# Windowed attention and a gated feed-forward on one core: two heads in one full-array matmul over 64-key blocks

## The chip, the cores and the metric

The kernel runs on one core of one Trainium2 chip. The metric is the device time of one execution in microseconds (us): the median of three runs. A profile of one execution is taken beside it, on the same chip, and all views quoted below are read from that trace.

## The reference, cut to what matters

Attention over 8 batches, 8 heads, 576 tokens and 64 dimensions a head, with two kinds of causal window, and then a gated feed-forward over all 4608 tokens:

```python
scores = scale * np.matmul(q, k.transpose(0, 1, 3, 2))
rel = pos[:, None] - pos[None, :]
mask_plain = (rel >= 0) & (rel < 32)                       # heads 0 to 3
mask_dil = (rel >= 0) & (rel < 128) & (rel % 4 == 0)       # heads 4 to 7
scores = np.where(mask, scores, -1e9)
attn = exp(scores - max); attn = attn / sum(attn)
attn_out = np.matmul(attn, v)                              # 8 x 8 x 576 x 64
x = attn_out.transpose(0, 2, 1, 3).reshape(4608, 512)
g = x @ w_gate                                             # 512 -> 1536
val = x @ w_val
return (gelu(g) * val) @ w_out                             # 1536 -> 512
```

A query of a plain head sees itself and the 31 tokens before it. A query of a dilated head sees every fourth token, 32 of them: sorted into four classes by position modulo 4, it sees itself and the 31 before it in its own class of 144 tokens. So most of the 576 x 576 scores of a head need not be computed.

## The kernel before

The tokens go through the feed-forward in nine blocks (`c`) of 512. A block has a gate stage, 96 matmuls of 512 columns (12 groups `nb` of 8), and an output stage, 48 matmuls (four rows of tokens `tb`, twelve terms `fc`). The attention of later batches is woven into these stages: `n` counts pairs of heads, four to a batch (two plain, two dilated), 32 in all. For each pair there is a score stage (`emit_s`), an exponential on ScalarE, a mask multiply on VectorE, and a value stage (`emit_pv`) with the denominators (a matmul with ones) and the numerators. Then VectorE transposes the denominators in 32x32 squares, takes reciprocals of one column of each, transposes them back and scales the numerators into `xT`, the feed-forward's input.

The two heads of a pair stand in the two halves of the array. In the score stage they use the upper and the lower 64 rows, as a head has 64 dimensions; in the value stage the left and the right 64 columns:

```python
def emit_s(n, b0, pe_mask=False):
    ...
    if is_plain(n):
        ...                                   # pe_mask: the mask as a bias, by matmuls with the identity
        for j in (0, 1, 2, 3, 4):             # 128-key blocks, 160 queries each
            for hl in range(2):
                kt = qtp_[64 * hl : 64 * hl + 64, 1, hp, :]
                qt = qtp_[64 * hl : 64 * hl + 64, 0, hp, :]
                ...
                mm(ps[:, bank, c0 : c0 + w], kt[:, k0 : k0 + P], qt[:, q0 : q0 + w], ...)
        nc.scalar.activation(pt[:, :, 0:PB], ..., AF.Exp, ...)          # 960 columns
        nc.scalar.activation(pt[:, :, PB:PH], ..., AF.Exp, ...)         # 384 columns
    else:
        ...                                   # 12 matmuls in halves: 8 of 128 columns, 4 of 32
        nc.scalar.activation(pt, ps[:, b0 : b0 + 4, 0:DW], AF.Exp, ...) # 1152 columns
    def emit_mask():
        nc.vector.tensor_tensor(pt, pt, mb, ALU.mult)

def emit_pv(n, b0, parts=("den", "num"), wide=False, flip=False):
    ...                                       # about 20 matmuls with 64 weight columns each
    for o, lhs, rhs, st in mms:
        nc.tensor.matmul(o, lhs, rhs, start=st, stop=True, skip_group_check=True)

def emit_both(n, b0):                         # plain pairs in a gate stage: values and ones side by side
    for hl in range(2):
        for j in range(5):
            ...                               # 128 weight columns: 64 of values, 64 of ones
            nc.tensor.matmul(ps[...], trio[:, hl : hl + 2, :]..., pt[:, hl, p0 : p0 + w], ...)
```

A batch is loaded two blocks ahead: plain q, k and v as float32 by the sync engine's queue and cast by GpSimd; the dilated parts by GpSimd's own queue, which casts on the way; then q and k are turned by DMA transposes:

```python
def load_batch_rest(b):
    st, sv = tiles["plain", b]
    qd, rd = load_qk_dil(b)
    qp = cast_qk_plain(b, st)
    load_v_dil(b)
    v_cast(b, sv)
    ...
    nc.sync.dma_start_transpose(out=dst[:, :, 0:P], in_=qd...)
    nc.sync.dma_start_transpose(out=dst[:, :, P:NCL], in_=rd...)
    for kb in range(5):
        nc.sync.dma_start_transpose(out=..., in_=qp[0:n, kb]...)
    last_keys(b, 0, HK, nc.gpsimd)
```

Which pair stands where is given by small tables. The plain pairs of batches 4 to 7 and the last dilated ones have their value stages in gate stages (`values_a`), the others in output stages (`values_b`):

```python
scores = {1: range(8, 12), 2: range(12, 17), 3: range(17, 22), 4: range(22, 27), 5: range(27, 32)}
values_b = {1: range(8, 12), 2: range(12, 16), 3: range(17, 20), 4: range(22, 24), 5: range(27, 28)}
values_a = {3: {4: 16}, 4: {2: 20, 6: 21}, 5: {1: 24, 4: 25, 7: 26}, 6: {1: 28, 4: 29, 7: 30, 10: 31}}
biased = (9,)
```

Of the kernel before, what the change touches and what calls it, by code (L numbers as in the profile page):

```python
# [21 lines left out]
def kernel(  # L22
# [14 lines left out]
    P = 128  # L37
# [13 lines left out]
    PB = 3 * PW  # L51
    PH = PB + P + PT
# [6 lines left out]
    qtp = ctx.enter_context(tc.tile_pool(name="qtp", bufs=2))  # L59
    prb = ctx.enter_context(tc.tile_pool(name="prb", bufs=8))  # L60
    nrm = ctx.enter_context(tc.tile_pool(name="nrm", bufs=2))
    ffn = ctx.enter_context(tc.tile_pool(name="ffn", bufs=3))
    osbp = ctx.enter_context(tc.tile_pool(name="osbp", bufs=4))
# [4 lines left out]
    mask_p = const.tile([P, PH], F16, tag="mask_p")  # L68
    mask_d = const.tile([P, DW], F16, tag="mask_d")
    bias_p = const.tile([P, PH], F16, tag="bias_p")  # L70
    bias_d = const.tile([P, DW], F16, tag="bias_d")
# [7 lines left out]
    vset = [  # L79
        (  # L80
            const.tile([P, 4, HP, 3, D], F16, tag=f"vp{i}", name=f"vp{i}"),
            const.tile([P, HK, 4, D], F16, tag=f"vd{i}", name=f"vd{i}"),
            const.tile([P, HP, 3, D], F16, tag=f"vt{i}", name=f"vt{i}"),
            const.tile([P, HK, 2, D], F16, tag=f"vr{i}", name=f"vr{i}"),
        )
        for i in range(3)
    ]
# [100 lines left out]
    def new_qt(b):  # L188
        tiles["qT", b] = (
            qtp.tile([P, 2, 2, S], F16, tag="qTp", name=f"qTp{b}"),  # L190
            qtp.tile([P, 2, HK, 2, NCL], F16, tag="qTd", name=f"qTd{b}"),
            qtp.tile([P, HK, 2, 64], F16, tag="kTr", name=f"kTr{b}"),
        )

    def new_v(b):

        sv = ldp.tile([P, 5, HK, D], F32, tag="sv", name=f"sv{b}")
        tiles["v", b] = vset[b % 3]
        return sv
# [18 lines left out]
    def load_qk_plain(b):  # L218
        st = ldp.tile([P, 5, 2, HK, D], F32, tag="st", name=f"st{b}")
        for t, src in ((0, q), (1, k)):  # L220
            for kb in range(5):
                n, sr = rows(src, b, kb)
                gated(nc.sync.dma_start(out=st[0:n, kb, t], in_=sr))
        return st

    def cast_qk_plain(b, st):
        qp = ldp.tile([P, 5, 2, HK, D], F16, tag="qp", name=f"qp{b}")
        nc.gpsimd.tensor_copy(qp[:, 0:4], st[:, 0:4])  # L228
        nc.gpsimd.tensor_copy(qp[0:64, 4], st[0:64, 4])
        return qp  # L230

    def load_qk_dil(b):
        qd = ldp.tile([P, 2, HK, 4, D], F16, tag="qd", name=f"qd{b}")
        rd = ldp.tile([16, 2, HK, 4, D], F16, tag="rd", name=f"rd{b}")
        for t, src in ((0, q), (1, k)):
            nc.gpsimd.dma_start(out=fl(qd[:, t]), in_=quads(src, b, HK, 0, 4 * P))
        for t, src in ((0, q), (1, k)):
            nc.gpsimd.dma_start(out=fl(rd[:, t]), in_=quads(src, b, HK, 4 * P, S))
        return qd, rd

    def load_eights(b):
        q8 = ldp.tile([R8, 2, HK, 8, D], F16, tag="qd", name=f"qd{b}")
        for t, src in ((0, q), (1, k)):
            tiles["last"] = nc.gpsimd.dma_start(
                out=q8[:, t].rearrange("p h r d -> p h (r d)"), in_=eights(src, b, HK, H)
            )
        return q8
# [12 lines left out]
    def load_batch_plain(b):  # L260
        st = load_qk_plain(b)
        sv = new_v(b)
        v_plain(b, sv, nc.sync)
        return st, sv

# [4 lines left out]
    def load_batch_rest(b):  # L270
        st, sv = tiles["plain", b]
        qd, rd = load_qk_dil(b)
        qp = cast_qk_plain(b, st)
        load_v_dil(b)
        v_cast(b, sv)
        new_qt(b)
        qtp_, qtd_, _ = tiles["qT", b]
        dst = qtd_.rearrange("p t h m i -> p (t h m) i")
        nc.sync.dma_start_transpose(out=dst[:, :, 0:P], in_=qd.rearrange("p t h r d -> p (t h r d)"))
        nc.sync.dma_start_transpose(out=dst[:, :, P:NCL], in_=rd.rearrange("p t h r d -> p (t h r d)"))  # L280
        dst = qtp_.rearrange("p t h c -> p (t h) c")
        for kb in range(5):
            n = min(P, S - kb * P)
            nc.sync.dma_start_transpose(
                out=dst[:, :, kb * P : kb * P + n], in_=qp[0:n, kb].rearrange("p t h d -> p (t h d)")
            )
        last_keys(b, 0, HK, nc.gpsimd)

# [51 lines left out]

    def emit_s(n, b0, pe_mask=False):
# [5 lines left out]
        if is_plain(n):  # L349
# [18 lines left out]
            pt = prb.tile([P, 2, PH], F16, tag="P", name=f"P{n}")  # L368
# [4 lines left out]
        else:  # L373
# [17 lines left out]
            pt = prb.tile([P, 4, DW], F16, tag="P", name=f"P{n}")  # L391
# [82 lines left out]
    def emit_both(n, b0):  # L474


        b, hp = n // NHP, n % 2
        pt = tiles["P", n]
        vp, _, vt, _ = tiles["v", b]
        for hl in range(2):  # L480
            for j in range(5):
                w = (PW, PW, PW, P, PT)[j]
                p0 = j * PW - (32 if j == 4 else 0)
                trio = vp[:, j, hp] if j < 4 else vt[:, hp]
                nc.tensor.matmul(
                    ps[:, b0 + 2 * hl + j // 4, j % 4 * P : j % 4 * P + w],
                    trio[:, hl : hl + 2, :].rearrange("p x d -> p (x d)"),
                    pt[:, hl, p0 : p0 + w],
                    start=j in (0, 4),
                    stop=True,  # L490
                    skip_group_check=True,
                )

    def both_rows(half, b0, hl):
        return psf[64 * half : 64 * half + 64, (b0 + 2 * hl) * 512 : (b0 + 2 * hl) * 512 + S]

    def norm_both_r(n, b0):
        dt = nrm.tile([P, 18, 32], F32, tag="dt", bufs=1)
        for hl in range(2):
            nc.vector.transpose(  # L500
                dt[64 * hl : 64 * hl + 64].rearrange("p b c -> p (b c)"), both_rows(1 - hl, b0, hl)
            )
        recip(n, dt)

    def norm_both_x(n, b0):
        b = n // NHP
        rb = tiles.pop(("rb", n))
        for hl in range(2):
            half = slice(64 * hl, 64 * hl + 64)
            nc.vector.tensor_tensor(  # L510
                xT[pair(n)][half, b * S : (b + 1) * S], both_rows(hl, b0, hl), rb[half], ALU.mult
            )

# [52 lines left out]
    def norm_parts(n, b0, at):  # L566

        for q0, q1 in ((0, at), (at, S)):
            dt = nrm.tile([P, 18, 32], F32, tag="dt", bufs=1)
            dt = dt[:, 0 : (q1 - q0) // 32]  # L570
            c0 = b0 * 512 + 960
            nc.vector.transpose(dt.rearrange("p b c -> p (b c)"), psf[:, c0 + q0 : c0 + q1])
            recip(n, dt)
            dst = xT[pair(n)][:, n // NHP * S + q0 : n // NHP * S + q1]
            num = psf[:, b0 * 512 + q0 : b0 * 512 + q1]
            nc.vector.tensor_tensor(dst, num, tiles.pop(("rb", n))[:, 0 : q1 - q0], ALU.mult)
# [82 lines left out]

    for vp_, _, vt_, _ in vset:  # L660
        nc.vector.memset(vp_.rearrange("p j g x d -> p (j g) x d")[:, :, 1, :], 1.0)
        nc.vector.memset(vt_[:, :, 1, :], 1.0)
# [11 lines left out]
    first_vd = ldp.tile([P, HK * 4 * D], F32, tag="st", name="st0")  # L674
    nc.sync.dma_start(out=fh(first_vd), in_=quads(v, 0, HK, 0, 4 * P))
    q6 = ldp.tile([R6, 2, 6, HK, D], F16, tag="qp", name="qp0")
# [57 lines left out]
    st1 = ldp.tile([R6, 2, HK, 6 * D], F32, tag="st", name="st1")  # L734
# [7 lines left out]
    q61 = ldp.tile([R6, 2, 6, HK, D], F16, tag="qp", name="qp1")  # L742
    for hp in range(2):
        for t in range(2):
            cast_six("pool", q61, st1, t, hp)
    gate["dma"] = wo1
    v_plain(1, sv1, nc.sync)
    v_cast(1, sv1)
    tiles["plain", 2] = load_batch_plain(2)

    mm0 = 0

    scores = {1: range(8, 12), 2: range(12, 17), 3: range(17, 22), 4: range(22, 27), 5: range(27, 32)}
    values_b = {1: range(8, 12), 2: range(12, 16), 3: range(17, 20), 4: range(22, 24), 5: range(27, 28)}
    values_a = {3: {4: 16}, 4: {2: 20, 6: 21}, 5: {1: 24, 4: 25, 7: 26}, 6: {1: 28, 4: 29, 7: 30, 10: 31}}
    biased = (9,)

    places = {
        1: "0.0m 1.3v 1.3s 1.3x 1.3m 2.5v 2.5s 2.5x 2.5m 3.0s 3.0m 3.6v 3.6x 3.12w",
        2: "0.0m 1.3v 1.3s 1.3x 1.3m 2.5v 2.5s 2.5x 2.5m 3.0s 3.0m 3.6v 3.6s 3.6x 3.12w 3.12m",
        3: "0.0m 1.3v 1.3s 1.3x 1.3m 2.5v 2.5s 2.5x 2.5m 2.11s 2.11m 3.6v 3.6s 3.6x 3.6m",
        4: "0.0m 1.3v 1.3s 1.3x 1.3m 2.4v 2.4s 2.4x 2.4m 2.11s 2.11m 3.7s 3.7m",
        5: "0.0m 1.3v 1.3s 1.3x 1.3m 2.1s 2.1m 2.10s 2.10m 3.6s 3.6m",
    }
    places = {c: [(int(w[0]), int(w[2:-1]), w[-1]) for w in p.split()] for c, p in places.items()}
    late = False
    for c in range(NCH):  # L770
# [87 lines left out]
        else:  # L858
# [39 lines left out]
            if lone:  # L898
                gelu_table()
# [36 lines left out]
```

The softmax here doesn't subtract the row's maximum and nothing guards it: scores larger than these inputs give would overflow.

## Time and profile before

| What | Value |
|---|---|
| Device time, median of 3 runs (lowest to highest) | 348.68 us (348.41 to 349.46) |
| Gate matmuls, 128x512, one of the two matrices | x432, 114.0 us busy |
| Output matmuls, 128x512 | x420, 96.9 us busy |
| Exponential, dilated pair, 1152 columns | 1130 ns |
| Exponential, plain pair, 960 and 384 columns | 970 and 488 ns |
| Mask multiply, dilated and plain pair | 751 and 856 ns |
| Transposes of denominators and of reciprocals, 576 columns | 778 ns each |
| Scaling into xT, dilated and plain pair | 1129 and 749 ns |
| DMA transposes of q and k on the sync queue (dilated, its rest, plain) | x6, x6, x30 |

Line numbers (L584) are those of the kernel printed above: L584 is a gate matmul, L618 an output matmul, L360 and L390 are scores, L472 and L485 values. "PE" is TensorE's matmuls, "PEld" its weight loads, "DVE" VectorE, "ACT" ScalarE, "POOL" GpSimd, "SPq" the sync engine's DMA queue. In a timeline a line has the start in us, the length in us, engine, line, operation, shapes and count. The length of a matmul contains its way through the array, so matmuls overlap one another; the distance between starts is what one costs.

### The profile page before, as it was taken

To read this page: it belongs to the slowest core of one execution; us is meant where nothing else is said; L and a number is where in the kernel's file an instruction comes from. 1 tells how busy PE (TensorE), PEld (TensorE's weight loads), DVE (VectorE), ACT (ScalarE), POOL (GpSimd) and SP (SyncE) were. 2 spreads that over 40 slices of the span, in tenths; PEclk is the share of its full clock that TensorE was granted. 3 is DMA by queue.
4 is the path that set the end of the run, shared out by engine and by line. 5 is a ranking of instruction groups with operands and counts; after the bars stand their busy time and mean duration, and the time that the engine had idled before them with its cause. 6 is when DMAs were issued, how large, how long until landed. Compare 5 with 4: busy or idle time off the path is not lost.

```text
span 347.0 us, 6006 instructions
## 1 busy us (share of the span) xinstructions
PE 336.0 (97%) x2342; PEld 163.7 (47%) x2342; DVE 201.8 (58%) x309; ACT 148.2 (43%) x220; POOL 84.0 (24%) x123
## 2 busy tenths in 40 slices
PE   8879999999999999999999999999999999999996
PEld 3644454444544445444544454444444444444443
DVE  3784488443794359674878576975498423303320
ACT  1753473535543447336553547336633223223321
POOL 8893304630630540351006300510000000000000
PEclk9999999999999999999999999999999999999999
DMA  8999999999999999898169925991100020020002
GB/s 179 225 201 223 205 200 192 184 147 258 178 107 256 191 152 171 201 162 121 62 159 168 157 73 137 195 126 55 70 0 0 32 91 1 2 91 30 2 30 91
DMA packets 107516, 44.44 MB, mean 128 GB/s; under 512 B 83328, under 2 KB 102912, under 8 KB 107488
## 3 DMA queue, kind: packets, MB, share of 16 engines
q1 hardware_dynamic: 84192, 31.01, 39.2%
q0 software_dynamic: 22752, 12.33, 28.9%
q10 hardware_dynamic: 544, 0.72, 0.8%
q8 instruction: 18, 0.29, 0.4%
q14 instruction: 10, 0.08, 0.1%
HBM read 39.85 MB, written 9.44 MB: 142 GB/s over the span
## 4 chain that ended last, share of the span: by engine, by line
PE 70%; DVE 13%; DMA 10%; issue 3%; ACT 2%; SPq 1%; POOL 1%; DVEq 0%; POOLq 0%; ACTq 0%
PE ps L584 42%; PE ps L618 21%; PE ps L472 4%; DMA st<-in_k_dram 4%; DMA sv<-in_v_dram 3%; DMA wv<-in_moe_w_val_dram 3%; DVE dt L500 2%; DVE dt L533 2%; DVE u_all L607 2%; DVE xT L559 2%; DVE rb L544 2%; DVE P L400 2%; DVE xT L510 1%; PE ps L390 1%; DVE rc L542 1%
## 5 line engine op out<-in xcount | busy, mean ns | idle before, releaser
L607 DVE SCALAR_TENSOR_TENSOR u_all<-g,ps 128x512 f16<-128x512 f16 x108 | 72.8, 684 | 76.7 <-PE ps L584 67.9
L606 ACT ACTIVATE g<-ps 128x512 f16<-128x512 f32 x108 | 63.9, 596 | 123.3 <-PE ps L584 122.8
L584 PE MATMUL ps<-xT,wg 128*128 128x512 f16 x432 | 114.0, 379 | 1.2 <-POOL xT L707 0.7
L584 PE MATMUL ps<-xT,wv 128*128 128x512 f16 x432 | 113.8, 379 | 0.2 <-DVE u_all L607 0.2
L618 PE MATMUL ps<-wo,u_all 128*128 128x512 f16 x420 | 96.9, 380 | 0.2 <-DVE qTd L303 0.2
L584 PEld LDWEIGHTS <-wv 128*128 128x128 f16 x432 | 42.2, 98 | 52.8 <-issue 2.9
L584 PEld LDWEIGHTS <-wg 128*128 128x128 f16 x432 | 41.3, 98 | 48.9 <-issue 1.1
L618 PEld LDWEIGHTS <-u_all 128*128 128x128 f16 x420 | 38.4, 98 | 44.7 <-issue 0.8
L629 ACT ACTIVATE osb<-ps 128x512 f32<-128x512 f32 x33 | 19.7, 597 | 38.8 <-PE ps L618 37.8
L228 POOL CAST qp<-st 128x2048 f16<-128x2048 f32 x6 | 11.4, 1893 | 97.8 <-DMA st<-in_k_dram 64.8
L544 DVE STREAM_TRANSPOSE rb<-rc 128x576 f32<-128x576 f32 (+4 forms) x34 | 25.3, 743 | 1.3
L533 DVE STREAM_TRANSPOSE dt<-ps 128x576 f32<-128x576 f32 x21 | 16.3, 778 | 12.4 <-PE ps L472 12.3
L392 ACT ACTIVATE P<-ps 128x1152 f16<-128x1152 f32 x16 | 18.1, 1130 | 11.8 <-PE ps L390 11.8
L370 ACT ACTIVATE P<-ps 128x960 f16<-128x960 f32 x16 | 15.5, 970 | 11.0 <-PE ps L360 11.0
L559 DVE TENSOR_TENSOR xT<-ps,rb 128x576 f16<-128x576 f32 x16 | 17.9, 1129 | 2.2 <-PE ps L472 1.9
L400 DVE TENSOR_TENSOR P<-P,mask_d 128x1152 f16<-128x1152 f16 x13 | 9.8, 751 | 9.7 <-ACT P L392 9.7
L400 DVE TENSOR_TENSOR P<-P,mask_p 128x1344 f16<-128x1344 f16 x14 | 11.8, 856 | 2.9 <-ACT P L371 2.9
L472 PE MATMUL ps<-P,ones 128*64 128x96 f16 (+5 forms) x174 | 11.3, 244 | 2.1 <-DVE P L400 1.5
L472 PEld LDWEIGHTS <-ones 128*64 128x64 f16 x174 | 7.2, 109 | 11.5 <-issue 8.6
L631 DVE TENSOR_SCALAR osb<-ps 128x512 f32<-128x512 f32 x2 | 1.4, 691 | 18.2 <-PE ps L618 18.2
L255 POOL DMA_DIRECT2D vr<-in_v_dram x16 | 9.9, 632 | 5.3 <-DMA wv<-in_moe_w_val_dram 3.6
L500 DVE STREAM_TRANSPOSE dt<-ps 64x576 f32<-64x576 f32 x14 | 10.9, 781 | 0.4
(88 smaller groups left out, 247.8 us busy)
## 6 DMA issues: line engine op xcount, KB each, us to landing
out_dram<-osb SPq DMA_DIRECT2D x35, 256.0 KB, 2.0
sv<-in_v_dram SPq DMA_DIRECT2D x40, 128.0 KB, 3.3
st<-in_q_dram SPq DMA_DIRECT2D x24, 128.0 KB, 3.1
st<-in_k_dram SPq DMA_DIRECT2D x24, 128.0 KB, 3.1
vd<-in_v_dram POOLq DMA_DIRECT2D x7, 256.0 KB, 6.5
wo<-in_moe_w_out_dram POOLq DMA_DIRECT2D x3, 512.0 KB, 19.7
qd<-in_q_dram POOLq DMA_DIRECT2D x6, 256.0 KB, 5.4
qd<-in_k_dram POOLq DMA_DIRECT2D x6, 256.0 KB, 6.9
```

The costliest lines, as they stand in the source:

```text
L392: nc.scalar.activation(pt, ps[:, b0 : b0 + 4, 0:DW], AF.Exp, bias=0.0, scale=scale)
L400: nc.vector.tensor_tensor(pt, pt, mb, ALU.mult)
L472: nc.tensor.matmul(o, lhs, rhs, start=st, stop=True, skip_group_check=True)
L500: nc.vector.transpose(dt[64 * hl : 64 * hl + 64].rearrange("p b c -> p (b c)"), both_rows(1 - hl, b0, hl))
L533: nc.vector.transpose(dst, den)
L544: nc.vector.transpose(rb[:, 0 : 32 * nb].rearrange("p (b c) -> p b c", c=32), bass.AP(tensor=rc.tensor, offset=rc.offset, ap=[rc.ap[0], [1 ...
L559: nc.vector.tensor_tensor(dst.rearrange("p (i m s) -> p i m s", m=2, s=2), num, rb.rearrange("p (s m i) -> p i m s", s=2, m=2), ALU.mult,)
L584: nc.tensor.matmul(ps[:, bank, :], w[:, kc, ns], xT[kc][:, tok], start=first, stop=end)
L606: nc.scalar.activation(g, ps[:, banks[0], :], AF.Gelu)
L607: nc.vector.scalar_tensor_tensor(u_all[:, nb, :], g, USCALE, ps[:, banks[1], :], ALU.mult, ALU.mult)
L618: nc.tensor.matmul(ps[:, bank, :], u_all[:, fc, tb * P : (tb + 1) * P], wo_t[fc // 4][:, fc % 4, :], start=(fc == 0), stop=(fc == NNB - 1),)
L629: nc.scalar.activation(osb, ps[:, bank, :], AF.Copy, bias=0.0, scale=1.0 / USCALE)
```

## The change

For batches 2 to 7 a pair's two heads go through the array together. The keys come in blocks of 64. A weight tile has one head's 64 keys in its first 64 columns and the other's in the last, each over its own 64 rows, and zeros in the other two quarters; so one matmul on the full array gives both heads' scores. Values are laid out the same way, and a matrix of ones in two diagonal squares gives the denominators. This takes less masked area (96 queries to 64 keys where it was 160 to 128), one exponential and one mask multiply of 832 or 768 columns to a pair, and no half-array form. Batches 0 and 1 keep the old form.

```diff
+    BK, BQ = 64, 96
+    LP, LD = 8 * BQ + BK, 4 * (BQ + 80) + BK
...
+    def two_s(n, bank):
...
+        for e, c0, t0, w in two_blocks(n):
+            if is_plain(n):
+                mm(c0, w, kp[:, 2 * e + hp, :], qp[:, hp, t0 : t0 + w])
+            else:
+                r = e % 4
+                mm(c0, w, kd[:, e, :], qd[:, hp, r, t0 - NCL * r : t0 - NCL * r + w])
+        if not is_plain(n):
+            mm(LD - BK, BK, kd[:, 16 + hp, :], qd[:, hp, :, P:NCL])
+        pt = prb.tile([P, LP], F16, tag="P", name=f"P{n}")
+        nc.scalar.activation(pt[:, 0:ln], psf[:, base : base + ln], AF.Exp, bias=0.0, scale=scale)
...
+    def two_m(n):
+        nc.vector.tensor_tensor(pt, pt, mask, ALU.mult)
...
+    def two_den(n, i):
+        two_mms(n, win(n, i), None)              # ones; several blocks in one matmul
+    def two_num(n, i):
+        ...                                      # one matmul a block, two where a bank ends
```

All loads of these batches now go through the sync engine's queue as float32, into a stage of three parts that is used twice a batch, and GpSimd casts them into the block-diagonal tiles; keys are transposed with their zeros:

```diff
+    def load_first(b):
+        load_q_plain(b, 0)                       # 6 loads
+        load_two(k, b, 1, True)                  # 4
+        load_q_dil(b, 2)                         # 1
+        cast_q_plain(b, 0)
+        cast_two(k16[:, 0], 1)
+        load_two(k, b, 0, False)                 # 6
+        cast_q_dil(b, 2)
+        cast_two(k16[:, 1], 0)
+    def load_rest(b):
+        if b < 5:
+            zero(blocks(vraw[b % 3], 1)), zero(blocks(vraw[b % 3], 0))
+        turn(qp..., q16[:, 0:1280])              # 10 blocks of 128 columns
+        turn(kp, k16[:, 0]...)                   # 18
+        load_two(v, b, 1, True)                  # 4
+        cast_two(vp, 1)
+        turn(qd..., q16[:, 1280:2304])           # 8
+        load_two(v, b, 2, False)                 # 6
+        cast_two(vd, 2)
+        turn(kd, k16[:, 1]...)                   # 18
+        nc.gpsimd.tensor_copy(qd[:, :, :, P:NCL], ...)
```

(The counts behind # are added here.) The tables are replaced by a list for each stage. A number is so many feed-forward matmuls; S, M, D, N are scores, mask, denominators and numerators of a pair; T is the first transpose with the reciprocal, B the second transpose, X the scaling; g and u are the two halves of the gating, e a store. What follows @ is the window in PSUM that the stage uses:

```diff
-    values_a = {3: {4: 16}, 4: {2: 20, 6: 21}, 5: {1: 24, 4: 25, 7: 26}, 6: {1: 28, 4: 29, 7: 30, 10: 31}}
+    gates = {
...
+        3: (
+            "G 2 T15 2 N15@1 e3@2 1 B15 3 X15 4 D16@0 N16@1 T16 2 g0 2 g1 1 u0 2 u1 2 g2 1 B16 3 u2 3 X16 1 g3 4 "
+            "u3 4 g4 4 u4 ..."
+        ),
...
+    outs = {
+        1: (
+            "9 S8@0 11 e0@1 M8 2 S9@0 1 D8@0 N8@1 T8 2 e1@1 1 S10@0 M9 1 B8 3 D9@0 X8 2 S11@0 M10 2 T9 N9@1 3 M11 "
+            "e2@1 1 D10@0 B9 2 T10 4 X9 2 N10@0 1 B10 1"
+        ),
+        2: (
+            "1 u11 6 S12@2 11 e0@2 M12 2 S13@2 1 D12@1 N12@0 T12 3 S14@2 M13 e1@2 1 B12 3 D13@1 X12 2 S15@2 M14 2 "
+            "T13 N13@0 3 M15 1 D14@1 B13 e2@2 S16@2 T14 5 X13 1 N14@1 1 B14 2 D15@0 M16 2 X14 1"
+        ),
...
```

So values that stood in the middle of gate stages now stand in output stages and in the first part of the gate stage after, and a store's fourth part (e3) of a block is issued in the next block, behind the loads of a batch. Masks, stages and tiles of probabilities share memory with others (the first batches' probabilities lie in the unused end of `xT`), and there are three output buffers in place of four.

## The prediction

> **What bounds the kernel now.** I read the busy shares first, then the table by stage, then the chain of waits piece by piece, then single stretches of TensorE's timeline, and last the DMA queue that the sync engine issues. The page says who is full:
>
> ```profile
> span 347.0 us, 6006 instructions
> PE 336.0 (97%) x2342; PEld 163.7 (47%) x2342; DVE 201.8 (58%) x309; ACT 148.2 (43%) x220; POOL 84.0 (24%) x123
> PEclk9999999999999999999999999999999999999999
> ```
>
> TensorE is busy 97% of the span at its full granted clock, so a time can only fall if TensorE gets less to do or idles less. How much of either there is, the last two blocks show. They hold no attention work, and the chain of waits has them as bare matmul stretches:
>
> ```profile
> 281.44 20.80 PE ps L584 x96
> 302.24 10.36 PE ps L618 x48
> ```
>
> One block of 512 tokens costs 20.80 + 10.36 = 31.16 us of feed-forward matmuls, 144 of them at 0.216 us. Nine blocks are 280.4 us and the change touches none of them. What it can touch lies in blocks 1 to 6. From TensorE's timeline I took where each block's first gate matmul starts (62.1, 98.9, 136.7, 173.9, 210.9, 247.5, 281.4) and asked for the table by stretch:
>
> ```profile
> 62.10:98.90 36.80, 36.56 (x276) 17.65 (x272) 20.27 (x29) 17.05 (x25) 14.62 (x19) 1.00 1.15 181
> 98.90:136.70 37.80, 36.90 (x284) 17.81 (x278) 23.27 (x37) 18.52 (x29) 12.00 (x17) 1.00 0.99 182
> ...
> 173.90:210.90 37.00, 36.26 (x261) 17.80 (x260) 26.99 (x39) 18.18 (x27) 8.85 (x12) 1.00 0.72 135
> ...
> sum 219.30, PE 216.62 PEld 105.27 DVE 143.83 ACT 100.65 POOL 50.67; mean PE 36.10 PEld 17.55 DVE 23.97 ACT 16.77 POOL 8.45
> ```
>
> The columns are length, then busy time of TensorE, its weight loads, VectorE, ScalarE and GpSimd. The six blocks take 219.3 us. Six times 31.16 is 187.0, so batches 2 to 7 cost 32.3 us beside the feed-forward: 219.3 - 216.6 = 2.7 us idle and 29.6 us of attention on TensorE. That is the whole pot, 9% of the time.
>
> Next, how attention is paid for now. Four lines of TensorE's timeline around one score and one value stage in half arrays:
>
> ```profile
> 157.84 1.03 PE L584 MATMUL ps<-xT,wv 128*128 128x512 f16 x4
> 158.79 0.47 PE L360 MATMUL ps<-qTp 64*128 64x160 f16 x10
> 159.19 3.41 PE L618 MATMUL ps<-wo,u_all 128*128 128x512 f16 x15
> 162.53 0.56 PE L472 MATMUL ps<-P,ones 128*64 128x64 f16 x10
> ```
>
> And three lines of it around a value stage on the full array:
>
> ```profile
> 145.16 1.03 PE L584 MATMUL ps<-xT,wv 128*128 128x512 f16 x4
> 146.03 0.43 PE L485 MATMUL ps<-P,vp 128*128 128x160 f16 x4
> ...
> 146.61 1.03 PE L584 MATMUL ps<-xT,wg 128*128 128x512 f16 x4
> ```
>
> Durations overlap, so starts are to be subtracted. From 157.84 to 158.79 are 0.95 us for four matmuls worth 0.86: entering the half-array form costs 0.09 us. From 159.19 to 162.53 are 3.34 us for fifteen worth 3.24: again 0.10. On the full array, from 145.16 to 146.03 are 0.87: nothing. The ten plain score matmuls (1344 columns) take 159.19 - 158.79 = 0.40 us, less than the 0.57 us that 1344 columns cost at 0.423 ns (0.2167 us over 512), so the two halves do run side by side. The full-array value stage runs 1344 columns in 0.58 us, exactly at that rate.
>
> **What the Trainium skill says.** "TensorEngine Tiling (Array Packing)", Tiling Modes, says that independent tiles work in parallel but that changing the tiling mode drains the engine; the trace agrees with both, 0.40 us against 0.57 for the parallel part and 0.09 to 0.10 us for the drain. "TensorE: Matmul & The Clock Gate", Back-to-back issue gap, gives about 81 ns per 128-column matmul with its own weight load in a stream; this trace differs, since ten matmuls of 134 columns on average took 58 ns each, and it decides. "VectorE: DVE Perf Modes", section on mode 2x_1P, allows two 16-bit results a cycle for a two-tensor operation on packed data; the mask multiplies agree (1152 columns in 751 ns, 1344 in 856: 0.55 ns a column and 0.12 fixed), so a shorter mask is worth what its columns are.
>
> **The change part by part.** A 64-key block with its two heads block-diagonal has 832 columns for a plain pair (eight of 96, one of 64), 768 for a dilated pair (four of 96, four of 80, 64 for the rest), each for scores, denominators and values.
>
> Price of a small full-array matmul. The page has no 96-column one with 128 weight columns, so I estimate from the transposes: twelve of 96 columns between 43.56 and 44.17 us, less a drain of 0.1, are 42 ns; twenty-four of 72 columns between 13.40 and 14.28 are 37 ns. I take 42 ns for 96, 40 for 80, 37 for anything shorter, and 0.423 ns a column where several blocks share one matmul (the denominators).
>
> - Plain pair: scores 8 x 42 + 37 = 0.37; denominators 832 x 0.423 = 0.35; values, where a bank border cuts one block, 7 x 42 + 3 x 37 = 0.41. Sum 1.13 us.
> - Dilated pair: scores 4 x 42 + 4 x 40 + 37 = 0.37; denominators 768 x 0.423 = 0.33; values 0.33 + 2 x 37 = 0.40. Sum 1.10 us.
> - Twelve of each: 26.8 us, in place of 29.6. TensorE saves 2.8 us.
>
> Where the 2.8 come from: the score stages drop from 0.49 (0.40 + 0.09) and 0.46 to 0.37 each, 24 x 0.105 = 2.5; the plain value stages in halves drop from 0.90 (0.80 + 0.10) to 0.76, five of them, 0.7; the four bias matmuls of one pair go, 0.6; the seven plain value stages that were already on the full array get dearer, 0.58 to 0.76, minus 1.3; dilated values stay (0.74 before with the drain, 0.73 now). The sum is 2.5, near the 2.8 by subtraction. This is the point of the estimate: zeros are multiplied now, and the parallel halves were worth nearly as much as the drains they cost.
>
> VectorE. A plain pair now costs mask 832 columns 0.58, transpose 0.78, reciprocal 0.27, transpose 0.78, scaling 0.76: 3.2 us; a dilated one 0.54 and 1.13 in place of 0.58 and 0.76: 3.5. The seven pairs of the gate stages cost 0.86 + 1.59 + 0.27 + 0.78 + 1.53 = 5.0 before. Over all, about 7 x 1.8 + 17 x 0.2 = 16 us less of VectorE, off the path except at the tight places. ScalarE's exponential goes from 1.13 or 1.35 us to about 0.85. Neither engine becomes the bound over a block (27 busy us of 37 at most before).
>
> Tight places stay. Between one pair's denominators and the next pair's values in the same two banks, VectorE needs 0.78 + 0.27 + 0.58 + 0.78 + 1.13 = 3.5 us and five hand-overs; the new lists put eleven 0.216-us matmuls and four small stages of 0.35 to 0.41 between, 3.9 us. At a block's end a queued transpose (0.78) can come on top. So I expect idle of some tenths at two or three places in a block, about as much as the 2.7 us in all of before.
>
> Start, block 0, blocks 7 and 8: same matmuls, same order. I put 0.
>
> Sum: 348.7 - 2.8 on TensorE, and 0.5 less for the lighter VectorE, against 0.5 to be expected from late data (below): about 345.8.
>
> **The rivals.** First, data come late. The sync engine's queue is in order, and it shows what one batch costs it now:
>
> ```profile
> 211.75 0.33 SPq L633 DMA_DIRECT2D out_dram<-osb  x1
> 212.13 2.81 SPq L223 DMA_DIRECT2D st<-in_q_dram  x5
> 215.32 3.39 SPq L223 DMA_DIRECT2D st<-in_k_dram  x5
> 218.82 2.75 SPq L204 DMA_DIRECT2D sv<-in_v_dram  x5
> 221.73 2.70 SPq L279 DMA_TRANSPOSE qTd<-qd  x1
> ```
>
> A load takes 0.56 us to issue, a transpose 2.70 for 16 blocks of 128 columns, 0.17 a block. The change needs 27 loads and 54 blocks of transposes a batch: 15.1 + 9.1 = 24.2 us, with the dilated keys last, and the page's 7.1 us until a wide transpose lands. The queue can begin some 3.5 us before a block starts, since the fourth store of a block is now issued behind the loads; so the last keys land about 28 us after the block's start, more if a load waits for a GpSimd cast in the shared stage. The first dilated score that needs them in block 5 (S30) comes after 20.8 us of gates, 30 output matmuls (6.5) and some 4 us of attention: 31 us. The margin is 3 us there, the like in block 4, and in block 1 about 2: batch 2's loads begin at 50.4 us now, end at about 75, land at 82, and S8 stands nine matmuls into the output stage, at 84.8. A late start of 2 us in all three would make 351; each alone 347 to 348. For it speaks that no margin is wide; against it that the lists put S8 two matmuls later in block 1 than its like elsewhere, as if the landing was known.
>
> Second, VectorE takes over at block ends. If each of five blocks stalls at three pair borders for 0.4 us more than now, that is 6 us and gives back more than TensorE saves: 351. Against it: VectorE loses 16 us of work over these blocks.
>
> Third, small full-array matmuls run at their bare columns (96 columns in 40.6 ns, a border piece in 25), and the lists take out nearly all idle: attention is then 12 x (2496 + 2304) x 0.423 ns = 24.4 us, idle 1, and the time 348.7 - 5.2 - 1.7 = 341.8. This is the best that the parts allow, and it is just about 2%.
>
> Fourth, GpSimd: it now casts q, k and v of each batch in halves and clears block-diagonal tiles, by its rows for casts (1024 columns in 1.07 us) about 17 us a batch in place of 9. In a block of 36 us it isn't the bound; it only delays the transposes, which the first rival holds.
>
> **How range and chances follow.** The sum stands at 345.8 us, a gain of 0.8%. The third rival sets the low side, 341.5. Late data or VectorE stalls set the high side, 351. A gain over 2% means at most 341.7 us, for which nearly all idle must go and the matmuls must be at their columns: 0.07. A loss over 2% means 355.7, seven us of new waits beyond what is saved, both bad rivals at once: 0.10. Within 2%: 0.83.
>
> **What would show it.** In the changed profile: 96-column matmuls with starts 40 to 44 ns apart and no step of 0.1 us before them; TensorE's busy sum in blocks 1 to 6 less by about 3 us, its idle near 2.7; the mask at 0.58 and the exponential at 0.85 us. It is wrong if the small matmuls start over 50 ns apart (then attention grows by 4 us), if score matmuls wait for a transpose or for GpSimd, or if block 0 (62.1 us to its end) moves by more than half a us.

## The result, and the profile after

The changed kernel takes 363.09 us (median of 4 executions, 362.26 to 364.34) where the kernel before takes 348.75. The ratio is 1.0409, with a 95% interval of 1.0385 to 1.0434: slower by 4.1%, and far above the range of the prediction. The head of its page:

```profile
span 360.5 us, 5943 instructions
PE 337.2 (94%) x2264; PEld 168.3 (47%) x2264; DVE 186.6 (52%) x290; ACT 138.6 (38%) x208; POOL 123.9 (34%) x153
PEclk9999999899996999999999999999999999999999
PE 55%; DMA 16%; DVE 11%; SPq 8%; POOL 6%; issue 2%; ACT 0%; POOLq 0%; DVEq 0%; ACTq 0%
```

The last line is the chain of waits by engine. TensorE has 78 matmuls fewer and is busy no less than before; its clock falls twice; and the chain has TensorE for 55% of the span where it was 70%, with DMA and the sync queue in its place. The table of blocks 1 to 6 again, the stretches between the blocks' first gate matmuls:

```profile
62.70:103.20 40.50, 36.42 (x234) 17.85 (x229) 19.23 (x28) 16.94 (x25) 26.46 (x36) 0.96 0.97 204
103.20:150.30 47.10, 38.80 (x258) 19.29 (x257) 22.74 (x36) 16.42 (x24) 21.01 (x22) 0.93 0.89 193
150.30:187.40 37.10, 36.95 (x268) 19.22 (x267) 23.32 (x38) 16.17 (x24) 12.03 (x12) 1.00 0.77 164
...
sum 231.70, PE 218.10 PEld 109.86 DVE 127.76 ACT 91.71 POOL 83.51; mean PE 36.35 PEld 18.31 DVE 21.29 ACT 15.28 POOL 13.92
```

Blocks 1 and 2 are longer than before by 3.7 and 9.3 us; the others are within 0.7 us or better. So the loss is no price of the new attention, which all six blocks pay. Who ends TensorE's idle time is the first line of its waits (us in all, times, longest):

```profile
PE ps L771 <- ACT osb L816: 11.5, 2, 7.6
```

A gate matmul (L771) waits for ScalarE's copy of an output block to its buffer (L816), once 3.9 and once 7.6 us. Three engines' timelines tell the second one. TensorE, ScalarE, and the sync engine's queue:

```profile
106.12 0.59 PE L771 MATMUL ps<-xT,wg 128*128 128x512 f16 x2
114.32 1.44 PE L771 MATMUL ps<-xT,wv 128*128 128x512 f16 x3 [7.61 <-ACT osb L816]
```

```profile
100.06 0.60 ACT L816 ACTIVATE osb<-ps 128x512 f32<-128x512 f32 x1 [0.68 <-PE ps L805]
...
113.67 0.60 ACT L816 ACTIVATE osb<-ps 128x512 f32<-128x512 f32 x1 [11.50 <-DMA out_dram<-osb]
```

```profile
80.74 1.01 SPq L820 DMA_DIRECT2D out_dram<-osb  x2
81.80 2.30 SPq L284 DMA_DIRECT2D stage<-in_q_dram  x4
...
108.22 2.98 SPq L335 DMA_TRANSPOSE q<-k  x1
111.31 1.50 SPq L820 DMA_DIRECT2D out_dram<-osb  x3
```

Read them from below. From 81.80 to 111.2 us the queue issues the loads and transposes of batch 3. The first three output blocks of block 1 lie in the three buffers by 100.7 us, but their stores come next in that queue, at 111.31. ScalarE's fourth copy finds no buffer for 11.5 us, the fourth bank of PSUM stays full, and the gate matmul that wants the bank stands still. At the start of block 1 the same happens to block 0's fourth copy.

After each stop TensorE runs at half speed. Stretches of stop, slow and normal, with the granted clock third from the end:

```profile
63.40:67.40 4.00, 0.14 (x1) 0.00 (x0) 1.30 (x2) 0.58 (x1) 3.45 (x4) 0.94 1.11 252
67.40:70.40 3.00, 2.93 (x8) 1.06 (x8) 0.00 (x0) 1.50 (x3) 2.91 (x3) 0.52 1.20 226
...
114.30:118.50 4.20, 4.18 (x11) 1.48 (x11) 1.38 (x2) 1.19 (x2) 0.00 (x0) 0.55 0.85 187
118.50:121.50 3.00, 3.00 (x15) 1.37 (x14) 0.79 (x2) 1.19 (x2) 1.83 (x2) 1.00 0.98 190
```

3.0 us at 0.52 and 4.2 at 0.55 lose 1.4 + 1.9 = 3.3 us. With the 11.5 us of stop that is 14.8 us, against 14.3 between the two medians.

### The profile page after: what moved, and what is told of

Read it like the earlier page. It is cut to its first block, busy times and chain, and to the rows that moved or that the text cites. A ratio compares the mean times of both kernels' runs of the same rounds, so it can differ in the third digit from the quotient of the medians.

```text
span 360.5 us, 5943 instructions
## 1 busy us (share of the span) xinstructions
PE 337.2 (94%) x2264; PEld 168.3 (47%) x2264; DVE 186.6 (52%) x290; ACT 138.6 (38%) x208; POOL 123.9 (34%) x153
## 4 chain that ended last, share of the span: by engine, by line
PE 55%; DMA 16%; DVE 11%; SPq 8%; POOL 6%; issue 2%; ACT 0%; POOLq 0%; DVEq 0%; ACTq 0%
PE ps L771 39%; PE ps L805 13%; DMA wo<-in_moe_w_out_dram 6%; DMA stage<-in_v_dram 5%; DVE xT L763 4%; DMA stage<-in_q_dram 3%; DVE dt L742 3%; DVE rb L750 2%; SPq L335 2%; SPq L219 2%; PE ps L724 2%; DVE P L670 1%; SPq L320 1%; SPq L284 1%; DMA out_dram<-osb 1%
## 5 line engine op out<-in xcount | busy, mean ns | idle before, releaser
L771 PE MATMUL ps<-xT,wv 128*128 128x512 f16 x432 | 116.1, 384 | 11.5 <-ACT osb L816 11.5
L771 PE MATMUL ps<-xT,wg 128*128 128x512 f16 x432 | 116.2, 383 | 1.8 <-DVE xT L763 0.9
L771 PEld LDWEIGHTS <-wv 128*128 128x128 f16 x432 | 42.0, 98 | 60.6 <-issue 13.1
L771 PEld LDWEIGHTS <-wg 128*128 128x128 f16 x432 | 42.5, 99 | 55.9 <-issue 7.0
L332 POOL CAST v<-stage 64x1152 f16<-64x1152 f32 x24 | 27.6, 1149 | 34.9 <-DMA stage<-in_v_dram 34.8
L816 ACT ACTIVATE osb<-ps 128x512 f32<-128x512 f32 x33 | 19.7, 596 | 50.7 <-PE ps L805 27.2
L332 POOL CAST k<-stage 64x1152 f16<-64x1152 f32 x24 | 27.7, 1154 | 9.8 <-DMA stage<-in_k_dram 9.4
L665 ACT ACTIVATE P<-ps 128x768 f16<-128x768 f32 (+1 forms) x24 | 20.1, 837 | 19.3 <-PE ps L654 19.0
L763 DVE TENSOR_TENSOR xT<-ps,rb 128x576 f16<-128x576 f32 x24 | 26.0, 1083 | 1.0
L750 DVE STREAM_TRANSPOSE rb<-rc 128x576 f32<-128x576 f32 x24 | 18.5, 772 | 0.2
L724 PEld LDWEIGHTS <-v 128*128 128x128 f16 x240 | 11.7, 98 | 4.8 <-issue 1.8
L724 PEld LDWEIGHTS <-two_ones 128*128 128x128 f16 x132 | 10.6, 97 | 7.2 <-issue 1.2
L654 PEld LDWEIGHTS <-q 128*128 128x128 f16 x216 | 11.3, 98 | 4.6
L724 PE MATMUL ps<-P,v 128*128 128x96 f16 (+3 forms) x240 | 12.6, 199 | 0.5 <-DVE xT L763 0.3
L276 POOL MEMSET v<- 64x1152 f16 x12 | 12.6, 1052 | 0.5
```

What stands on the lines that cost most here:

```text
L276: nc.gpsimd.memset(t[64 * x : 64 * x + 64, :, 64 - 64 * x : 128 - 64 * x], 0.0)
L332: nc.gpsimd.tensor_copy(dst[half, :, half], st[half])
L665: nc.scalar.activation(pt[:, 0:ln], psf[:, base : base + ln], AF.Exp, bias=0.0, scale=scale)
L750: nc.vector.transpose(rb.rearrange("p (b c) -> p b c", c=32), bass.AP(tensor=rc.tensor, offset=rc.offset, ap=[rc.ap[0], [1, 18], [0, 32]]),)
L763: nc.vector.tensor_tensor(dst, num, rb, ALU.mult)
L771: nc.tensor.matmul(ps[:, bank, :], w[:, kc, ns], xT[kc][:, tok], start=first, stop=end)
```

## The experiments

My theory: the three buffers, and the place of the stores behind a batch's loads in the one queue, make the whole loss, and the clock follows the stops. The rivals: **late data** (the queue carries too much, and without these waits the scores would wait for transposes); **clock** (the full-array form itself pulls the clock down); **too few buffers in any order**. A run's time is its median, its ratio that to the kernel before.

**Four buffers** (`four_buffers`):

```diff
-    osbp = ctx.enter_context(tc.tile_pool(name="osbp", bufs=3))
+    osbp = ctx.enter_context(tc.tile_pool(name="osbp", bufs=4))
```

> The changed kernel with four output buffers in place of three, nothing else. Theory (buffers): the fourth store of blocks 0 and 1 waits for a buffer whose own store stands behind a whole batch of loads in the sync engine's queue; with a fourth buffer TensorE's 3.9 and 7.6 us of idle at the starts of blocks 1 and 2 are gone, the granted clock, which fell only after them, is 1.000 throughout, and the time is 346 to 348.5 us. Rival (late data): the queue carries too much, so the same time is lost elsewhere, in score stages that wait for transposes: 355 us or more. Rival (clock): the full-array form itself pulls the clock down: mean clock stays below 0.99 and the time at 351 us or more.

Measured: 355.37 us, ratio 1.0222 (1.0171 to 1.0272). Half right. Both stops are gone, block 1 takes 35.4 us; but one of 6.2 us has come at the start of block 3 (in the execution with the profile, which at 358.66 us was the longest of four). TensorE and the queue there:

```profile
138.68 0.81 PE L771 MATMUL ps<-xT,wg 128*128 128x512 f16 x3
145.65 1.44 PE L771 MATMUL ps<-xT,wv 128*128 128x512 f16 x3 [6.16 <-ACT osb L816]
```

```profile
139.02 3.19 SPq L335 DMA_TRANSPOSE q<-k  x1
142.32 2.02 SPq L820 DMA_DIRECT2D out_dram<-osb  x4
```

Four stores leave at 142.32: the fourth of block 1, which the change put behind batch 4's loads, and three of block 2. The fourth of block 2 was a fifth one. The time is one that both rivals allow, but no score waited for a transpose, so late data isn't it; and the clock fell only behind the stop, to 0.50 from 145.6 to 151.4 us. Whether it needs the full-array form, the kernel before tells below.

**Stores from ScalarE's queue**, three buffers (`stores_on_act_queue`):

```diff
-        nc.sync.dma_start(out=out[t0 : t0 + P, :], in_=osb)
+        nc.scalar.dma_start(out=out[t0 : t0 + P, :], in_=osb)
```

> The changed kernel with its three buffers, but all stores issued from ScalarE's queue, so that none stands behind loads. Theory (buffers held behind loads): three buffers then suffice, no wait of ScalarE for a store over 1 us, 346 to 349 us. Rival (three buffers are too few by themselves, whatever the queue): the idle stays, 360 us or more. Rival (late data): 355 us or more, with waits in score stages.

Measured: 358.08 us, ratio 1.0286 (1.0244 to 1.0327). The expectation failed, and the run doesn't settle what it was made for. ScalarE's timeline in block 0:

```profile
53.90 0.59 ACT L816 ACTIVATE osb<-ps 128x512 f32<-128x512 f32 x1
63.24 0.37 ACTq L820 DMA_DIRECT2D out_dram<-osb  x1
63.71 0.60 ACT L816 ACTIVATE osb<-ps 128x512 f32<-128x512 f32 x1 [9.23 <-DMA stage<-in_k_dram]
```

The output block is ready at 54.5, its store is issued at 63.24, and what ends the wait by the trace is the landing of a load of keys. So by the trace a store issued from another engine was still tied to a load, and now ScalarE itself stood. (Loads were tied to stores as well: those of L320 waited for stores to land five times, 13.3 us in all.) What ties them the trace doesn't say; it stays open. One thing it does show: the stops at the starts of blocks 1 and 2 are gone with three buffers, and no copy of ScalarE waits more than 2.0 us for one. In their place TensorE stands behind ScalarE, 5.5 us in block 0 and 1.8 in block 1.

**The kernel before with three buffers** (`before_three_buffers`; the same line, 4 to 3):

> The kernel before with three output buffers in place of four. In its queue too the four stores of block 0 are issued only at 73.7 us, behind batch 2's loads and transposes. Theory: the fourth store's buffer then comes free at about 76 us, where TensorE needs its bank at about 63: 12 to 14 us of idle at the start of block 1, some us of low clock behind it, a smaller wait at block 2: 360 to 368 us. Rival (only the changed kernel's longer queue makes three too few): 348 to 351 us.

Measured: 369.92 us, ratio 1.0622 (1.0587 to 1.0656), a little above the range. TensorE at the start of block 1:

```profile
62.98 0.38 PE L584 MATMUL ps<-xT,wg 128*128 128x512 f16 x1
80.60 0.59 PE L584 MATMUL ps<-xT,wv 128*128 128x512 f16 x1 [17.25 <-ACT osb L629]
80.98 0.63 PE L584 MATMUL ps<-xT,wg 128*128 128x512 f16 x1
```

The old attention with its halves stops for 17.2 us, and its clock falls too: starts 0.38 us apart after the stop, and 0.43 later on. The wait at block 2 that I expected as well didn't come. So the fall of the clock needs no full-array attention, and of the old kernel's four buffers none was to spare.

**Scaling in row order**, four buffers (`four_buffers_scale_in_row_order`). VectorE's scaling of dilated pairs (L763) had become slower, 1.38 to 1.46 us where it was 1.13 (the 1.29 below is the part of one that lay on the chain of waits), so:

```diff
-            dst = dst.rearrange("p (i r) -> p r i", r=4)
-            num = num.rearrange("p (r i) -> p r i", r=4)
-            rb = rb.rearrange("p (r i) -> p r i", r=4)
+            dst = dst.rearrange("p (i r) -> p i r", r=4)
+            num = num.rearrange("p (r i) -> p i r", r=4)
+            rb = rb.rearrange("p (r i) -> p i r", r=4)
```

> Four buffers, and the scaling of dilated pairs walks xT in the order of its rows as the kernel before did, reading PSUM and the reciprocals with a step, where the change wrote xT with a step. Theory: this one operation falls from 1.29 to 1.46 us to about 1.13 as before, and the time by 0.3 to 1.5 us against four buffers alone, as the scaling stands in the chain at the ends of output stages. Rival (off the path): the operation shortens and the time stays within 0.2 us.

Measured: 352.99 us, ratio 1.0142 (1.0112 to 1.0173), 2.4 us under four buffers alone, more than I expected. The two ratios' intervals still touch, and the stop at block 3 was 0.6 us shorter in this trace (5.6 us); the same edit under five buffers is clearer, below.

**Loads behind the fourth store**, four buffers (`four_buffers_loads_behind`):

```diff
                 store(at, args[0], out_banks(at)[args[0]], "act" if kind == "e" else "dve")
+                if at == c - 1 and c + 2 < B:
+                    load_first(c + 2)
+                    load_rest(c + 2)
...
-        if 1 <= c and c + 2 < B:
+        if c == 1:
             load_first(c + 2)
             load_rest(c + 2)
```

> Four buffers, and in blocks 2 to 5 the loads of the next batch are issued behind the fourth store of the block before instead of ahead of it. Theory (store order): with four buffers alone 6.2 us of idle stood at block 3, where the fourth store of block 2 was a fifth one behind one batch's loads; now never more than four stores wait, no idle over 1 us is left, the clock stays at 1.000: 346.5 to 348.5 us. Rival (late data): the loads begin some 4 us later in each block, the last keys land behind the scores that need them, and score stages wait: 350 us or more.

Measured: 350.06 us, ratio 1.0039 (1.0026 to 1.0052). No wait for a buffer, clock 1.000. The time is above the range and just in that of the rival, but no score waited for a transpose. What TensorE waited for was VectorE's scaling, 4.2 us in ten places:

```profile
PE ps L724 <- DVE xT L763: 2.6, 7, 0.5
PE ps L771 <- DVE xT L763: 1.6, 3, 0.7
```

**The same in row order** (`four_buffers_loads_behind_row_order`):

> The same with the scaling in row order. Theory: the scaling gave 2.4 us with the idle still there; without the idle it gives 1 to 2.4, so 344.5 to 346.5 us, which is faster than the kernel before by about 1%. Rival (late data): 349 us or more.

Measured: 348.18 us, ratio 0.9989 (0.9973 to 1.0005): level with the kernel before and above the expected range. The waits for the scaling fall to 1.2 us, and now two score stages wait for transposes of keys, 1.2 us together. That is all that this trace shows of late data.

**Three buffers, loads behind** (`three_buffers_loads_behind`; the change as it stands and the last diff alone):

> The changed kernel with three buffers as it stands, only the loads of blocks 2 to 5 moved behind the fourth store. Theory (both are needed): the fourth store of a block needs the buffer of the first, whose store now stands behind the loads of the same block in every block, so the idle of blocks 1 and 2 stays (3.9 and 7.6 us) and others come: 362 to 372 us. Rival (the place of the fourth store alone was the fault): 350 us or less.

Measured: 363.73 us, ratio 1.0431 (1.0413 to 1.0450), with 10.3 us of waits for ScalarE's copies in two places, at the starts of blocks 1 and 2 as in the change (4.8 and 5.6 us). The others that I expected didn't come. The loads of batches 2 and 3, behind which these two stops' stores stand, are not among those that the edit moves; so the run shows that this order doesn't make three buffers enough, and no more. Other orders weren't tried.

**Five buffers, row order** (`five_buffers_row_order`):

```diff
-    prb = ctx.enter_context(tc.tile_pool(name="prb", bufs=7))
+    prb = ctx.enter_context(tc.tile_pool(name="prb", bufs=6))
...
-    osbp = ctx.enter_context(tc.tile_pool(name="osbp", bufs=3))
+    osbp = ctx.enter_context(tc.tile_pool(name="osbp", bufs=5))
```

> Scaling in row order and five buffers (the tiles of probabilities are six instead of seven to make room), the loads where the change put them, ahead of the fourth store. Theory (it is only the number of stores that can wait): five buffers hold the fourth store of the block before and all four of this one, so the order does no harm: 344.5 to 347 us, the same as loads behind with four. Rival (the queue falls behind for good): idle comes back in a later block: 349 us or more.

Measured: 347.12 us, ratio 0.9955 (0.9942 to 0.9968), just above the expected range and faster than the kernel before. With room for five stores the order of the change brings no stop. Its table of blocks 1 to 6:

```profile
62.00:97.40 35.40, 35.05 (x233) 17.53 (x228) 18.99 (x28) 16.41 (x25) 21.95 (x33) 1.00 1.04 201
97.40:135.20 37.80, 36.84 (x257) 18.89 (x256) 21.85 (x35) 16.31 (x24) 23.50 (x23) 1.00 0.99 204
...
sum 217.10, PE 214.52 PEld 109.24 DVE 125.67 ACT 91.11 POOL 84.07; mean PE 35.75 PEld 18.21 DVE 20.94 ACT 15.18 POOL 14.01
```

Against the sums of before (219.3, of them 216.6 busy) TensorE has 2.1 us less to do, and idles 2.6 us where it idled 2.7. (What one tile of probabilities less does by itself wasn't measured.)

**Controls.** The kernel before with five buffers (`before_five_buffers`):

> The kernel before with five output buffers in place of four. It never waited over 0.9 us for a buffer, so theory (its buffers were just enough): no change, 348 to 349.5 us, and what the changed kernel with five buffers gains over the kernel before, 1.6 us, is then due to the attention's form and order. Rival (a fifth buffer helps any kernel here): 347.5 us or less.

Measured: 349.09 us, ratio 1.0008 (0.9996 to 1.0020). A fifth buffer gives the old kernel nothing. The change with five buffers and its own scaling (`five_buffers`):

> The changed kernel with five output buffers (six tiles of probabilities), the scaling left as the change wrote it, with a step in xT. Theory: no idle for buffers, clock 1.000, and the step costs what it cost in the two pairs of runs before, 1.9 and 2.4 us over the row order: 348.7 to 349.7 us, that is no gain over the kernel before. Rival (the step costs only where idle hides elsewhere): 347.5 us or less.

Measured: 349.52 us, ratio 1.0024 (1.0008 to 1.0040); the step in the writes costs 2.4 us against the row order (1.9 against its repetition below), and here the intervals are apart. Five buffers, row order and the loads behind (`five_buffers_loads_behind_row_order`):

> Five buffers, row order, and the loads of blocks 2 to 5 behind the fourth store as well. With four buffers this order of loads left 1.2 us of waits of scores for transposes and 348.2 us. Theory (the loads' start is what it costs, not the buffers): the waits stay and the time is 347.5 to 348.7 us, above the 347.1 with the loads ahead. Rival (four buffers still cost something): 347.2 us or less.

Measured: 348.65 us, ratio 0.9995 (0.9982 to 1.0008), inside the range, but scores waited only 0.4 us for keys; and its interval overlaps that of the repetition below, so it isn't shown to be slower than with the loads ahead. The fastest version again (`five_buffers_row_order_again`):

> The fastest version once more with more rounds, since its first figure stands on few executions and its neighbours scatter by two to three us. Theory (it is faster than the kernel before): 346.8 to 347.8 us, ratio below 0.998 with its whole interval. Rival (its first figure was a lucky draw): 348 us or more.

Measured: 347.63 us, ratio 0.9974 (0.9958 to 0.9989). Its interval reaches over the 0.998 that I set and stays under 1. So the best version beats the kernel before by a quarter to half a per cent. The executions of the changed kernel's versions scatter over 3 to 4 us where there are 14 or more of them, those of the kernel before over less than 2; why wasn't found.

## Why the prediction was wrong

**The step that failed** is the sum's term for idle: "some tenths at two or three places in a block, about as much as the 2.7 us in all of before". Idle in blocks 1 to 6 was 13.6 us (231.7 - 218.1), 11.5 of it in the two stops, and the half clock behind them cost 3.3 us more. The sum had no term for the output buffers, though the diff held all of it: three buffers in place of four, and a block's fourth store behind the next batch's loads. I counted that move only as a gain, an earlier start for the queue. None of the signs of being wrong that I named is a wait for a buffer. The line "Start, block 0, blocks 7 and 8: same matmuls, same order. I put 0" did hold, but for half a us at each end: block 1 starts at 62.7 us where it started at 62.1, and the part from block 7 on takes 66.1 us where it took 65.6. (In versions without these two stops block 1 starts between 61.7 and 62.7, so the 0.6 us lie within the scatter.)

That the buffers are the cause is shown from both sides, with the stores in the loads' queue. Three of them stop the old kernel for 17.2 us; five take the changed one from 363.1 to 349.5 us (ratio 1.0409 to 1.0024), which is all but 0.8 of the loss, and a fifth gives the old kernel nothing.

**Late data**: the mechanism was right up to its victim. I put 24.2 us of queue for a batch; in block 1 it was 29.4 (81.80 to 111.2), and the queue's waits in that stretch name GpSimd for 6.8 us and TensorE for 1.3. The time until a transpose of keys landed was too high in return, 7.1 us where the median is 4.7. But I asked only which load lands late for which score, and not what else stands in that queue. The stores stood there. Scores waited little: 1.2 and 0.4 us where I started the loads later, and 0.6 us in the trace of the repeated fastest version, with the loads where the change put them:

```profile
131.95 0.54 PE L654 MATMUL ps<-q 128*128 128x96 f16 x9 [0.59 <-DMA q<-k]
```

**TensorE's work** was right in kind, and the saving a little smaller: 2.1 us in blocks 1 to 6 of the version without stops, where 2.8 were put. The prices of the new stages held. Nine score matmuls took 0.34 to 0.37 us from start to start of their neighbours against 0.37, with no step of 0.1 us ahead of them; summed in this way, the 24 score stages take 8.5 us and the denominators and values 17.9, where 8.9 and 17.9 were put. The busy sum has 27.5 us beside the feed-forward (214.5 - 187.0), 1.1 more than these two; where that lies wasn't taken apart.

**VectorE** loses 16.0 us in blocks 1 to 6 (143.8 to 127.8), as worked out, but by luck: one scaling operation of a dilated pair was put at 1.13 us and took 1.38 to 1.46, and with five buffers and row order, where it takes what was put, VectorE loses 18.2 us (125.7). Its line in the trace of the change and in that of five buffers with row order (shortest, median, longest ns):

```profile
L763 DVE TENSOR_TENSOR xT<-ps,rb x24: 696/1068/1455, 97.6 to 268.3; 128x576 f16<-128x576 f32 x24
```

```profile
L763 DVE TENSOR_TENSOR xT<-ps,rb x24: 695/893/1136, 91.7 to 253.1; 128x576 f16<-128x576 f32 x24
```

Writing with a step of four costs up to 1.46 us, reading with it 1.14, and as TensorE waits for this operation, the step in the writes was worth 1.9 to 2.4 us of the whole. The second rival, VectorE at block ends, was thus a true one, at a third to two fifths of the 6 us that I gave it as its worst.

**The estimate for a clean kernel**, 345.8 us, was a little low: 347.1 and 347.6 with five buffers and the scaling in row order. The third rival's 341.8 was not reached: it put 24.4 us of attention on TensorE and 1 us of idle, and that version has 27.5 and 2.6. Three small slips stand in the working: the sum's own terms make 345.9, the second rival's 6 us 351.8, and the margin in block 1 is 2.8 us by its figures.

## What to carry to other kernels

When a change lengthens an in-order queue or thins a pool of buffers, list everything that leaves by that queue, and count how many results must wait while the longest batch of loads goes out; the pool needs that many. Here one short stopped the engine that bounds the kernel, the old one by 17.2 us and the new one with four by 6.2. Each stop of TensorE of 3.9 us or more was paid twice here, by the stop and by the slow clock after it. Check the operand that is walked with a step in every operation at a stage's end: writing with the step cost more here than reading with it, 1.38 to 1.46 us against 1.03 to 1.14.

## What the runs showed of the hardware

After stops of 3.9, 6.2, 7.6 and 17.2 us TensorE's 512-column matmuls started 0.43 us apart in place of 0.216, for some 3 to 6 us; after a wait of 1.8 us (block 1, stores from ScalarE's queue) they kept 0.216. The Trainium skill, "TensorE: Matmul & The Clock Gate", Seeing it yourself, tells of a re-throttle 5.2 us after the last matmul in one run; here a stop of 3.9 us was followed by a granted clock of 0.52. I hadn't counted on it in any rival. And a store issued from ScalarE's queue waited 9.2 us, by the trace until a load issued by the sync engine had landed.
